# Reordered set-up loads, a split first value sum, TensorE transposes at the end and separate ranks for the first and last steps

## The chip, the cores and the metric

The kernel runs on one core of a Trainium2 chip. The metric is device time in microseconds (us) of one execution, as the median of eight runs. A core has five engines with a queue of instructions each: TensorE (PE in the profile; its weight loads are shown as PEld), VectorE (DVE), ScalarE (ACT), GpSimd (POOL) and SyncE (SP). All transfers of this kernel, the transposing ones too, are issued from SP's queue, one after the other.

## The reference, cut to what matters

Four layers are applied to a sequence of 2048 rows of width 448: A, B, A, B, each added to its input after a layer norm. A is attention with a recurrent memory over 64 segments of 32 rows; B is a gated product with ReLU.

```python
def A(x, mem, Wq, Wk, Wv, Wo):           # 16 heads of 256, 8 memory rows
    for s in range(64):
        h = concat(mem, x[32*s:32*s+32])              # 40 rows
        q, k, v = h @ Wq, h @ Wk, h @ Wv              # per head
        p = softmax(mask(q @ k.T / 16))
        o = (p @ v) @ Wo                              # summed over the heads
        mem = o[:8]                                   # carried to the next segment
        out[s] = o[8:]
def B(x, Wg, Wu, Wd):                    # 1792 wide inside
    return (relu(x @ Wg) * (x @ Wu)) @ Wd
x = x + A(norm(x)); x = x + B(norm(x)); x = x + A(norm(x)); x = x + B(norm(x))
```

Both A layers use the same weights and the same first memory, and so do both B layers.

## The kernel before

**Set-up.** Two products of weights are formed per head, so that no q, k or v is ever built: M = Wq Wk^T (448 x 448 per head, in the tiles `M` and `M3`) and N = Wv Wo (in `N`, 56 blocks of 128 x 448: three blocks of 128 rows for each of 16 heads, numbered `c * 16 + h`, and eight blocks, 48 to 55, that hold the last 64 rows of two heads). `setup` loads Wq, Wk and Wv in head quarters (four heads, 896 KB each) by transposing transfers (`wT`, line 661) and Wo by plain ones (`wo`, line 665), into eight slots of one large tile; Wv and Wo reuse the slots of Wq and Wk. `products` (a quarter at a time) issues the products on TensorE, and ScalarE and VectorE copy each result out of PSUM (`prodE`). The first memory goes through two small loads (lines 654 and 655), one transposing transfer (`mT`, line 656) and a copy on GpSimd (`start_mem`) into `hT`, from which all of step 0 hangs. The slots of the large tile later become the buffers `U` and `UR` and the weights of B.

**Steps.** Step t treats segment t of the first A layer and segment t - 4 of the second together, so there are 68 steps; the first four have the first layer alone and the last four the second alone. In a step, `t_units` multiplies the 40 rows of each layer by M, in ten groups (`tH0`..`tH4` for the last 64 of the 448 rows of the product's inner width, `tF0`..`tF4` for the rest). `s_mem` scores the eight memory rows (`smem`), softmax runs on DVE and ACT (`smx`), `p_t_mem` transposes the probabilities `Pm` on TensorE (`ptm`) and copies them to `PTm`, `u_mem` multiplies them by the rows (`umem`), and `un_mem` sums 56 blocks of N times `UTm` (`unm`, four column groups of the array side by side, 112 matmuls) into the new memory, which `m_t` (`mt`) puts into `hT` for step t + 1. That chain is the recurrence. Beside it, `s_seg` scores the other rows (`sseg`, softmax `ssx` into `Ps`), a transposing transfer (`pts`, line 878) makes `PTs`, `u_seg` multiplies (`useg0`..`useg3`), and `h_nat` supplies the rows in the other layout by a transfer (`hk`, line 884).

**Pairs.** After an odd step, `un` sums 56 blocks of N for the 64 rows of the pair (`un0`..`un3`, or `unc0`..`unc3` where only one layer has rows), `tile_q` normalises the rows (`ln_b`, with a transposing transfer `xBT<-xnB`, line 775) and runs B on them (`glu`: `glH`, `glF`, then the down product `dn` or `dnc`). The second layer's rows of every other pair travel with the memory rows of a later step (`ride`), so a round of four steps repeats: `un` at steps with t % 4 = 1 and `unc` at t % 4 = 3.

**Order.** The order on every engine is made at build time by `_Order.run`: a list scheduler that knows a cost for each operation, starts the one that can go next (within `SLACK` of the earliest), and prefers the highest rank. An operation's rank is its longest path to the end plus `BIAS[kind]`; for TensorE's operations it is a base that falls by 90000 every four steps, plus `BIAS`. `RESERVE[kind]` holds back PSUM banks, and `MODEPEN` is a penalty for a change of the array's tiling. TensorE's kinds carry the step's position in the round:

```python
    def mm(self, kind, fn, cost, rd, wr, mode=FULL):
        self.q.add(f"{kind}.{self.t % 4}", ("pe",), {"pe": (cost + 177.0, cost)}, fn, rd, wr, mode=mode, base=-PERIOD * (self.t // 4))
```

Waits are derived from the reads and writes of each operation, and a queue takes its instructions in the planned order.

Of the kernel before, what the change touches and what calls it, by code (L numbers as in the profile page):

```python
# [6 lines left out]
BF = dt.bfloat16  # L7
# [12 lines left out]
NSEG = 64  # L20
# [8 lines left out]
NP = (NSEG + LAG) // 2  # L29
NSTEP = NSEG + LAG  # L30
# [141 lines left out]
class _Order:  # L172
# [198 lines left out]
BIAS = {"dn.1": -135297.0, "dn.3": -206162.0, "dnE": -604.0, "dnc.1": -674.0, "dnc.3": -136569.0, "glE": -29394.0, "glF0.1": 606.0,  # L371
    "glF0.3": -174334.0, "glF1.1": -142301.0, "glF1.3": -117036.0, "glF2.1": -146133.0, "glF2.3": -132890.0, "glF3.3": -107953.0, "glH0.1":
    5303.0, "glH0.3": -121200.0, "glH1.1": -7321.0, "glH1.3": -104138.0, "glH2.1": -287.0, "glH2.3": -124319.0, "glH3.1": -32499.0,
    "glH3.3": -142572.0, "hk": -25670.0, "init": 17030.0, "lna": -21575.0, "lnaC": 10845.0, "lnaT": 21955.0, "lnb": -26144.0, "mt":
    -18205.0, "mt.0": -22219.0, "mt.1": -153718.0, "mt.2": -1981.0, "mt.3": -108880.0, "mtE": 1853.0, "prodE": 14190.0, "prodM.0":
    -107349.0, "prodN.0": 716.0, "ptm.0": -44820.0, "ptm.1": -17541.0, "ptm.2": -15676.0, "ptm.3": -2267.0, "ptmE": 1947.0, "pts": -1708.0,
    "ride": 22906.0, "rt": -1627.0, "rtT": -18816.0, "smem.0": -2247.0, "smem.1": -3879.0, "smem.2": 10512.0, "smem.3": -126055.0, "smx":
    36486.0, "sseg.0": -14434.0, "sseg.1": 704.0, "sseg.2": -85569.0, "sseg.3": -113319.0, "ssx": 5592.0, "tEm": -574.0, "tEs": -132155.0,
    "tF0.0": 7089.0, "tF0.1": -307.0, "tF0.2": -3560.0, "tF0.3": -18673.0, "tF1.0": 6620.0, "tF1.1": 432.0, "tF1.2": -390.0, "tF1.3":
    -103195.0, "tF2.0": -1468.0, "tF2.1": 9264.0, "tF2.2": 13111.0, "tF2.3": 522.0, "tF3.0": -15739.0, "tF3.1": 2809.0, "tF3.2": -14339.0,  # L380
    "tF3.3": -377.0, "tF4.0": -102794.0, "tF4.1": -105119.0, "tF4.2": 13464.0, "tF4.3": -138946.0, "tH0.0": 3809.0, "tH0.1": 769.0, "tH0.2":
    3829.0, "tH0.3": -14778.0, "tH1.0": 3745.0, "tH1.1": 5395.0, "tH1.2": -4790.0, "tH1.3": -58455.0, "tH2.0": 8825.0, "tH2.1": 8934.0,
    "tH2.2": 2440.0, "tH2.3": 7015.0, "tH3.1": 6664.0, "tH3.2": -373.0, "tH3.3": -115448.0, "tH4.0": -9140.0, "tH4.1": 571.0, "tH4.2":
    21710.0, "tH4.3": -783.0, "umE": -26170.0, "umem.0": 502.0, "umem.1": 7799.0, "umem.2": -1164.0, "umem.3": -14491.0, "un0.1": -1073.0,
    "un0.3": -109778.0, "un1.1": -141926.0, "un1.3": 8423.0, "un2.1": 1237.0, "un2.3": 50702.0, "un3.1": -1050.0, "un3.3": 5387.0, "unc0.1":
    -75505.0, "unc0.3": 3823.0, "unc1.1": -31084.0, "unc1.3": -441.0, "unc2.1": -97666.0, "unc2.3": -112127.0, "unc3.1": -113243.0,
    "unc3.3": -120926.0, "unm.0": -16096.0, "unm.1": -107910.0, "unm.2": 54678.0, "unm.3": -100930.0, "usE": -49724.0, "useg0.0": -76906.0,
    "useg0.1": 49445.0, "useg0.2": -108968.0, "useg0.3": 364.0, "useg1.0": -113562.0, "useg1.1": -97375.0, "useg1.2": -134407.0, "useg2.0":
    -97605.0, "useg2.1": -113.0, "useg2.2": -111646.0, "useg2.3": -127783.0, "useg3.0": -124837.0, "useg3.1": -57685.0, "useg3.2":
    -128034.0, "useg3.3": 3737.0, "w": -19731.0, "wg": -28478.0, "wo": -12799.0, "x": -7455.0, "xE": 41308.0, "xb": -17247.0, "yE": -4405.0,  # L390
    "ys": -6145.0}
RESERVE = {"dn.1": 2, "dn.3": 1, "dnc.1": 2, "dnc.3": 1, "glH0.1": 4, "glH0.3": 1, "glH1.1": 1, "glH1.3": 2, "glH2.1": 1, "glH2.3": 4,
    "glH3.1": 3, "mt.2": 1, "mt.3": 1, "prodM.0": 2, "prodN.0": 1, "ptm.0": 2, "ptm.1": 4, "ptm.2": 4, "ptm.3": 3, "smem.1": 4, "smem.2": 1,
    "smem.3": 2, "sseg.0": 2, "sseg.1": 4, "sseg.2": 4, "tH0.0": 1, "tH0.2": 1, "tH0.3": 2, "tH1.0": 4, "tH1.1": 1, "tH1.2": 2, "tH1.3": 2,
    "tH2.0": 4, "tH2.2": 1, "tH2.3": 2, "tH3.0": 2, "tH3.1": 1, "tH3.3": 1, "tH4.0": 2, "tH4.1": 2, "tH4.2": 3, "tH4.3": 4, "umem.0": 1,
    "umem.1": 3, "umem.2": 3, "un0.1": 3, "un0.3": 3, "unc0.1": 1, "unc0.3": 1, "unc1.1": 2, "unc1.3": 2, "unc2.1": 2, "unc2.3": 2,
    "unc3.1": 2, "unc3.3": 2, "unm.2": 3, "useg0.0": 1, "useg0.1": 2, "useg0.3": 2, "useg1.0": 2, "useg1.1": 1, "useg1.2": 1, "useg1.3": 3,
    "useg2.0": 1, "useg2.1": 3, "useg2.2": 4, "useg2.3": 2, "useg3.0": 2, "useg3.1": 3, "useg3.2": 1, "useg3.3": 2}
SLACK = {"pe": 101.0, "act": 139.0, "dve": 229.0, "pool": 332.0, "sp": 256.0}
PERIOD = 90000.0  # L400
MODEPEN = 41401.0
# [25 lines left out]
def TR(out, src, ident):  # L427
    return (out, src, ident, dict(is_transpose=True))
# [6 lines left out]
class _Kernel:  # L435
# [133 lines left out]
    def mm(self, kind, fn, cost, rd, wr, mode=FULL):  # L569

        self.q.add(f"{kind}.{self.t % 4}", ("pe",), {"pe": (cost + 177.0, cost)}, fn, rd, wr, mode=mode, base=-PERIOD * (self.t // 4))
# [78 lines left out]
    def setup(self):  # L650
        S = self
        S.dma("x", "x0", lambda E: E.dma_start(S.XA[0:64, 0, :], S.x_d[0:64, :]), (), [("XA", 0, 0)])
        mN = S.gT[0:16, :, :].rearrange("p a b -> p (a b)")[:, 0:640]
        S.dma("x", "mN0", lambda E: E.dma_start(mN[0:8, 0:448], S.mem_d), (), [("gT", 0)])
        S.dma("x", "mN1", lambda E: E.dma_start(mN[0:8, 576:640], S.mem_d[:, 384:448]), (), [("gT", 1)])
        S.dma("x", "mT", lambda E: E.dma_start_transpose(S.mTc[:, :, :], mN), [("gT", 0), ("gT", 1)], [("mTc",)], 1160.0, 2400.0)
# [3 lines left out]
        def wT(k, W, q, slow=0.0):  # L660
            S.dma("w", f"w{k}", lambda E: E.dma_start_transpose(S.slot[k], W[:, q * 1024:(q + 1) * 1024]), (), [("slot", k)], 3900.0 + slow,  # L661
                  6200.0 + 1.4 * slow)

        def wo(k, q):
            S.dma("wo", f"w{k}", lambda E: E.dma_start(S.slot[k], S.Wo_d[:, q * 8:q * 8 + 8, :]), (), [("slot", k)], 620.0, 5800.0)
# [36 lines left out]
        for q in range(4):  # L702
            wT(2 * q, S.Wq_d, q)
            wT(2 * q + 1, S.Wk_d, q)
        for q in range(4):
            products(q, 2 * q, 2 * q + 1, True)
        for q in range(4):
            wT(2 * q, S.Wv_d, q, 2300.0 if q else 0.0)
            wo(2 * q + 1, q)
# [7 lines left out]
        for k in range(3):  # L717
            S.dma("wg", f"Wg{k}", lambda E, k=k: E.dma_start(S.Wg[:, k, :], S.Wg_d[k * 128:k * 128 + 128, :]), S.big_keys("Wg"), [("Wg", k)], 500.0, 3000.0)
            S.dma("wg", f"Wu{k}", lambda E, k=k: E.dma_start(S.Wu[:, k, :], S.Wu_d[k * 128:k * 128 + 128, :]), S.big_keys("Wu"), [("Wu", k)], 500.0, 3000.0)
# [465 lines left out]
```

## Time and profile before

| what | us |
|---|---|
| median of 8 runs (lowest, highest) | 1542.08 (1538.39, 1547.73) |
| the profiled execution | 1540.43 |
| its span, first to last instruction | 1538.4 |
| PE busy in the span | 1473.8 |
| ACT busy, DVE busy | 811.0, 698.7 |
| first product of the set-up starts on PE | 10.85 |
| first `un_mem` ends | 86.5 |
| first sum of `unc`'s form (step 3) starts | 137.80 |
| last sum of `un` ends | 1521.6 |

Matmuls overlap in the array, so a PE that is shown busy is not always at its peak. The median is what is forecast; the execution in the profile was 1.65 us faster than it.

### The profile page before, as it was taken

What the parts mean: (1) busy time and instruction counts of PE and PEld (TensorE: products, weight loads), DVE (VectorE), ACT (ScalarE), POOL (GpSimd) and SP (SyncE); (2) the same over time, 40 slices, a digit from 0 to 9 for tenths busy, and PEclk for the clock granted to TensorE, in tenths of its full rate; (3) what the DMA queues carried; (4) which work ended last, traced back from release to release, by engine and by line L of the source; (5) the groups of instructions that cost most, each with busy time, mean ns of one, the idle gap of its engine ahead of it and who ended that gap; (6) DMA issues with size and microseconds to landing.
All of it is one profiled execution on the core that took longest, in us unless ns stands there. A gap on an engine that the chain in (4) does not pass through costs nothing.

```text
span 1538.4 us, 72169 instructions
## 1 busy us (share of the span) xinstructions
PE 1473.8 (96%) x33352; PEld 1157.5 (75%) x33352; DVE 698.7 (45%) x1851; ACT 811.0 (53%) x2421; POOL 90.9 (6%) x142
## 2 busy tenths in 40 slices
PE   5789999999999999999999999999999999999998
PEld 2467777887878778887877778787877788787775
DVE  4334444443535455344535454344535444353443
ACT  5544545555555646555555545555554555545543
POOL 2000000000000000000000000000000000000000
PEclk9999999999999999999999999999999999999999
DMA  9851111011111111111112112111112201221111
GB/s 222 179 146 33 23 29 28 19 29 29 32 20 34 25 32 26 23 29 29 29 24 34 24 26 29 23 33 28 29 21 34 28 19 29 28 31 19 31 26 23
DMA packets 187549, 59.76 MB, mean 39 GB/s; under 512 B 176344, under 2 KB 186352, under 8 KB 187248
## 3 DMA queue, kind: packets, MB, share of 16 engines
q1 hardware_dynamic: 187248, 55.15, 19.7%
q8 instruction: 262, 4.29, 1.2%
q14 instruction: 39, 0.32, 0.1%
HBM read 10.33 MB, written 1.84 MB: 8 GB/s over the span
## 4 chain that ended last, share of the span: by engine, by line
PE 87%; DMA 6%; DVE 3%; ACT 2%; SPq 1%; issue 1%; POOL 0%; POOLq 0%
PE P L134 87%; DMA PTs<-Ps 4%; DMA xBT<-xnB 1%; SPq L661 1%; ACT big L599 1%; DMA mTc<-gT 1%; ACT XH L943 0%; DMA big<-in_A_Wk_dram 0%; DVE X L946 0%; DMA stg<-xnA 0%; DVE xnB L757 0%; DVE stat L823 0%; DVE stat L820 0%; DVE big L600 0%; DVE hB L1077 0%
## 5 line engine op out<-in xcount | busy, mean ns | idle before, releaser
L134 PE MATMUL P<-hT,Mw 128*128 128x80 bf16 (+1 forms) x11424 | 422.3, 200 | 0.4 <-ACT Mw L599 0.4
L134 PEld LDWEIGHTS P<-hT,Mw 128*128 128x128 bf16 x11424 | 403.2, 100 | 9.3 <-ACT Mw L599 0.5
L134 PE MATMUL P<-Nw,big 128*64 128x448 bf16 (+1 forms) x1904 | 283.7, 353 | 0.5
L599 ACT ACTIVATE TTm<-P 128x96 bf16<-128x96 f32 (+2 forms) x612 | 147.9, 242 | 239.3 <-PE P L134 231.1
L599 ACT ACTIVATE TTs<-P 128x384 bf16<-128x384 f32 (+2 forms) x596 | 268.6, 451 | 0.2
L134 PE MATMUL P<-xBT,big 128*128 128x128 bf16 (+3 forms) x3808 | 213.9, 217 | 3.0 <-DMA xBT<-xnB 3.0
L134 PEld LDWEIGHTS P<-Nw,big 128*64 128x64 bf16 (+1 forms) x1904 | 136.1, 104 | 107.0 <-issue 3.4
L134 PEld LDWEIGHTS P<-xBT,big 128*128 128x128 bf16 (+1 forms) x3808 | 182.9, 98 | 24.8 <-issue 10.2
L134 PE MATMUL P<-Nw,UTm 128*32 128x224 bf16 x7504 | 193.6, 261 | 2.8 <-ACT UTm L599 2.8
L134 PEld LDWEIGHTS P<-Nw,UTm 128*32 128x32 bf16 x7504 | 176.2, 97 | 20.5 <-issue 11.5
L599 ACT ACTIVATE big<-P 128x512 bf16<-128x512 f32 (+1 forms) x371 | 176.4, 536 | 23.4 <-PE P L134 22.4
L820 DVE TENSOR_REDUCE stat<-P 128x8 f32<-128x320 f32 (+3 forms) x135 | 46.2, 351 | 212.3 <-PE P L134 212.0
L600 POOL COPY UTm<-big 128x896 bf16<-128x896 bf16 x56 | 52.3, 934 | 1109.2 <-PE P L134 1109.2
L600 DVE CAST TTm<-P 128x64 bf16<-128x64 f32 (+3 forms) x68 | 15.5, 228 | 198.1 <-PE P L134 197.9
L946 DVE TENSOR_TENSOR X<-P,XH 32x224 bf16<-32x224 f32 x134 | 51.1, 381 | 116.4 <-ACT XH L943 113.7
L600 DVE CAST big<-P 128x512 bf16<-128x512 f32 (+1 forms) x141 | 90.3, 655 | 27.5 <-PE P L134 25.3
L134 PE MATMUL P<-PTs,hK 64*128 64x512 bf16 (+1 forms) x640 | 84.2, 337 | 18.9 <-DMA PTs<-Ps 15.3
L134 PE MATMUL P<-big,hB 128*128 128x448 bf16 (+1 forms) x476 | 98.7, 353 | 1.5 <-DVE hB L1077 1.5
L134 PE MATMUL P<-hT,M 64*128 64x80 bf16 (+1 forms) x3808 | 92.4, 196 | 7.8 <-POOL hT L600 6.2
L1076 ACT ACTIVATE gT<-P 128x512 bf16<-128x512 f32 (+2 forms) x136 | 70.7, 522 | 51.9 <-PE P L134 47.6
L134 PEld LDWEIGHTS P<-hT,M 64*128 64x128 bf16 x3808 | 74.7, 96 | 30.7 <-issue 11.7
L1077 DVE TENSOR_TENSOR hB<-gT,P 128x512 bf16<-128x512 bf16 (+2 forms) x136 | 76.5, 589 | 41.8 <-PE P L134 37.6
(85 smaller groups left out, 1155.6 us busy)
## 6 DMA issues: line engine op xcount, KB each, us to landing
big<-in_A_Wo_dram SPq DMA_DIRECT2D x4, 896.0 KB, 6.9
XA<-in_A_x_dram SPq DMA_DIRECT2D x32, 56.0 KB, 2.4
out_dram<-ys SPq DMA_DIRECT2D x32, 56.0 KB, 2.0
big<-in_B_W_down_dram SPq DMA_DIRECT2D x2, 784.0 KB, 9.3
big<-in_B_W_gate_dram SPq DMA_DIRECT2D x3, 448.0 KB, 5.0
big<-in_B_W_up_dram SPq DMA_DIRECT2D x3, 448.0 KB, 6.6
PTs<-Ps SPq DMA_TRANSPOSE x68, 2.6
hK<-hT SPq DMA_TRANSPOSE x68, 2.6
```

The costliest lines, as they stand in the source:

```text
L134: ins = E.matmul(out, lhsT=lhsT, rhs=rhs, **kw)
L599: return E.activation(out(), src(), ACT.Copy)
L600: return E.tensor_copy(out(), src())
L661: S.dma("w", f"w{k}", lambda E: E.dma_start_transpose(S.slot[k], W[:, q * 1024:(q + 1) * 1024]), (), [("slot", k)], 3900.0 + slow, 6200.0 ...
L820: S.dve(kind, lambda E: E.tensor_reduce(st[:, so:so + n], src(), AX.X, ALU.max), w, rd, [(pre, 0)])
L946: S.dve("xE", lambda E, r=r, r2=r2, c=c: E.tensor_tensor(S.X[r, c], T.b()[r, 0:224], S.XH[r2, :], ALU.add), 224, T.res((j,)) + [("XH",)], ...
L1076: S.act("glE", lambda E, G=G, k=k, w=w: E.activation(S.gT[:, k % 2, 0:w * n], G.b()[:, 0:w * n], ACT.Relu), w * n, G.res(), [("gT", k % 2)])
L1077: S.dve("glE", lambda E, V=V, k=k, w=w, a=a: E.tensor_tensor(S.hB[:, a:a + w, 0:n], S.gT[:, k % 2, 0:w * n].rearrange("p (i x) -> p i x", ...
```

## The change

Four edits, and new values in all tables of the scheduler.

1. In `setup`, x0, the two memory loads and the memory's transposing transfer get a kind of their own (`mem`) with a high rank. Each of the 16 weight loads has its own kind (`wq0`..`wo3`), and the costs that the scheduler assumes for transfers are altered.
2. The first `un_mem` (t = 0) is issued as four operations over head quarters. Each waits for the 14 blocks of N of its quarter instead of all 56. The other steps sum in the same new order of blocks, in one operation.
3. The last `PTs<-Ps` (step 67) and the last `xBT<-xnB` (pair 33) are no longer transfers: four transposes on TensorE into one PSUM bank and one copy on VectorE.
4. Kinds on TensorE are numbered 4 to 7 in steps 0 to 3, 8 to 11 in steps 64 to 67, and 0 to 3 in between.

```diff
-BIAS = {"dn.1": -135297.0, "dn.3": -206162.0, "dnE": -604.0, "dnc.1": -674.0, "dnc.3": -136569.0, "glE": -29394.0, "glF0.1": 606.0,
...
+BIAS = {"dn.1": -104633.0, "dn.3": -214049.0, "dn.9": -140910.0, "dnE": -786.0, "dnc.11": -139309.0, "dnc.3": 13831.0, "dnc.5": -27812.0,
...
-SLACK = {"pe": 101.0, "act": 139.0, "dve": 229.0, "pool": 332.0, "sp": 256.0}
+SLACK = {"pe": 101.0, "act": 142.0, "dve": 226.0, "pool": 0.0, "sp": 124.0}
 PERIOD = 90000.0
-MODEPEN = 41401.0
+MODEPEN = 42065.0
...
-        self.q.add(f"{kind}.{self.t % 4}", ("pe",), {"pe": (cost + 177.0, cost)}, fn, rd, wr, mode=mode, base=-PERIOD * (self.t // 4))
+        part = 4 if self.t < 4 else 8 if self.t >= NSEG else 0
+        self.q.add(f"{kind}.{self.t % 4 + part}", ("pe",), {"pe": (cost + 177.0, cost)}, fn, rd, wr, mode=mode, base=-PERIOD * (self.t // 4))
...
-        S.dma("x", "x0", lambda E: E.dma_start(S.XA[0:64, 0, :], S.x_d[0:64, :]), (), [("XA", 0, 0)])
+        S.dma("mem", "x0", lambda E: E.dma_start(S.XA[0:64, 0, :], S.x_d[0:64, :]), (), [("XA", 0, 0)])
...
-        S.dma("x", "mN0", lambda E: E.dma_start(mN[0:8, 0:448], S.mem_d), (), [("gT", 0)])
-        S.dma("x", "mN1", lambda E: E.dma_start(mN[0:8, 576:640], S.mem_d[:, 384:448]), (), [("gT", 1)])
-        S.dma("x", "mT", lambda E: E.dma_start_transpose(S.mTc[:, :, :], mN), [("gT", 0), ("gT", 1)], [("mTc",)], 1160.0, 2400.0)
+        S.dma("mem", "mN0", lambda E: E.dma_start(mN[0:8, 0:448], S.mem_d), (), [("gT", 0)])
+        S.dma("mem", "mN1", lambda E: E.dma_start(mN[0:8, 576:640], S.mem_d[:, 384:448]), (), [("gT", 1)])
+        S.dma("mem", "mT", lambda E: E.dma_start_transpose(S.mTc[:, :, :], mN), [("gT", 0), ("gT", 1)], [("mTc",)], 1200.0, 2500.0)
...
+        if q == NP - 1:
+            S.transposed("lnbT", S.xnB[:, :], 512, S.xBT[:, :, :].rearrange("p a b -> p (a b)"), [("xnB",), ("xnB", 0), ("xnB", 1)], [("xBT",)])
+            return
...
+        if t == NSTEP - 1:
+            S.transposed("pts", S.Ps[:, :, :].rearrange("p a b -> p (a b)"), 512, S.PTs[:, :, :].rearrange("p a b -> p (a b)"), [("Ps",)], [("PTs",)])
+            return
...
+    def transposed(self, kind, src, n, dst, rd, wr):
+
+        S = self
+        T = S.tile()
+        S.mm(kind, lambda: [TR(T.b().bitcast(BF)[:, c:c + 128], src[:, c:c + 128], S.ident[:, :]) for c in range(0, n, 128)],
+             n // 128 * S.pitch(128), rd + [("ident",)], T.res())
+        S.cp(kind + "E", lambda: dst, lambda: T.b().bitcast(BF)[:, 0:n], n, T.res(), wr, speed=1.9, eng=("dve",))
...
+    OS = [[c * 16 + h for c in range(3) for h in range(4 * q, 4 * q + 4)] + [48 + 2 * q, 49 + 2 * q] for q in range(4)]
...
+        rd = [("UTm", 0), ("UTm", 1), ("UTmr",)]
+        if t == 0:
+            for q in range(4):
+                S.mm("unm", lambda q=q: mms(7 * q, 7 * q + 7), 7 * S.pitch(224), rd + [("N", o) for o in S.OS[q]], T.res(), mode=COLS4)
+        else:
+            S.mm("unm", lambda: mms(0, 28), 28 * S.pitch(224) + 18.0, rd, T.res(), mode=COLS4)
```

## The prediction

> **What bounds the kernel now.** I read the page's busy times and chain first, then what PE waited for, then the first 100 us and the last 20 us in fine windows.
>
> ```profile
> PE 1473.8 (96%) x33352; PEld 1157.5 (75%) x33352; DVE 698.7 (45%) x1851; ACT 811.0 (53%) x2421; POOL 90.9 (6%) x142
> ...
> PE 87%; DMA 6%; DVE 3%; ACT 2%; SPq 1%; issue 1%; POOL 0%; POOLq 0%
> ```
>
> PE holds 87% of the chain that ended last. Time can come off only where PE stands still, runs at half clock, or changes tiling needlessly. PE's waits over the whole span:
>
> ```profile
> PE P L134 <- DMA big<-in_A_Wk_dram: 15.9, 4, 10.9
> PE P L134 <- DMA PTs<-Ps: 15.3, 15, 1.9
> PE P L134 <- POOL hT L600: 6.2, 2, 5.8
> PE P L134 <- issue: 3.4, 3, 2.0
> ```
>
> (columns: total us, times, longest). The first line is the weights of the set-up, the third the first memory. The second is not the ends: 14 of its 15 waits lie between 140 and 1480 us, one in each round of four steps. Set-up, first SP's timeline (columns: start us, us, what):
>
> ```profile
> 33.13 0.52 SPq L654 DMA_DIRECT2D gT<-in_A_mem_dram  x1
> 36.78 3.96 SPq L656 DMA_TRANSPOSE mTc<-gT  x1
> 49.65 14.48 SPq L661 DMA_TRANSPOSE big<-in_A_Wv_dram  x3
> ```
>
> Then windows of 4 us (columns: PE, PEld, DVE, ACT, POOL busy, granted clock, DMA share, GB/s):
>
> ```profile
> 40.00:44.00 4.00, 0.00 (x0) 0.00 (x0) 0.07 (x1) 0.32 (x2) 0.00 (x0) 1.00 1.20 362
> 44.00:48.00 4.00, 2.50 (x30) 1.35 (x31) 0.23 (x1) 0.77 (x2) 0.22 (x1) 0.61 1.07 225
> 48.00:52.00 4.00, 3.56 (x98) 2.62 (x96) 0.67 (x3) 2.98 (x12) 0.00 (x0) 0.96 0.35 89
> 56.00:60.00 4.00, 1.95 (x10) 0.55 (x8) 0.78 (x2) 1.16 (x3) 0.00 (x0) 0.82 1.28 189
> ```
>
> The memory's transfer is issued at 36.78, behind 2.7 MB of Wo, and takes 8.4 us to land. PE has placed step 0's first units ahead of the last M products, so it stands still from 39.65 to 45.5. That also keeps a slot occupied: the last Wo waits for PE, and the DMA share falls to 0.35 at 48 to 52. The tail, by the timeline:
>
> ```profile
> 1524.57 1.31 PE L134 MATMUL P<-big,hB 128*128 128x448 bf16 x6 [1.51 <-DVE hB L1077]
> 1527.49 5.75 PE L134 MATMUL P<-xBT,big 64*128 64x64 bf16 x112 [1.61 <-DMA xBT<-xnB]
> ```
>
> and a window in it:
>
> ```profile
> 1527.00:1533.00 6.00, 5.51 (x111) 5.24 (x112) 1.23 (x4) 1.30 (x4) 0.00 (x0) 0.50 0.10 22
> ```
>
> Two gaps on PE, and the last gated products run at clock 0.50.
>
> **Set-up loads and the split sum.** From 35.95 (last quarter of M starts) to the end of the first `un_mem`, about 86.5, PE's windows leave 8.6 us idle: 0.35, 4.0, 1.5, 0.44, 2.05 and 0.29 in the windows from 36, 40, 44, 48, 56 and 64. Half clock adds 1.4 us (10 product matmuls in 3.18 us, where 64 later ones took 11.33, so 0.177 each) and 1.6 (24 in 5.89 against 4.25). That is 11.7 us; the work itself is about 39 us.
>
> With the memory first, the stall of 5.85 and its half clock go, and Wo3's hold-up with them. What is moved costs at the front: SP issues the two memory loads (0.52 and 0.28) and the transpose, before the bulk of the weights. The transpose's issue is between 1.2 (every small transpose at an uncrowded queue, such as `stg<-xnA` at 9.40) and 3.96 (where it is now); I take 1.2, because only one weight load is ahead of it. So Wq and Wk land 2.0 us later (bounds 0.8 and 4.8; below 0.8 only if the backlog on the queue hides an issue). This is paid in full: PE waited 1.7, 2.0 and 1.3 us for each next quarter, so nothing covers it. POOL's copy into `hT` then waits for no late transfer; on POOL's queue it stands behind memsets that end at 8.5.
>
> The split adds three waits and some tiling changes, 0.1 to 0.2 us each: 0.4. Its gain is bounded by the sum itself, 2.9 us, of which three quarters (2.1) can lie before the last N blocks. But PE is busy there (64 product matmuls without a gap, 71.20 to 82.5), so on a PE-bound stretch moving them brings nothing; it helps only in a wait for Wv. I book 0 for it: the cover is PE's own work, and without it the end is Wv3's arrival plus 5.6 of products.
>
> That arrival: DMA is full from 4 to 48 and from 52 to 66, idle for about 3 between. Without the hole the last weights land near 63 to 65. PE, from 38, with 5.3 of M, 5.3 of units and 16.6 of N, wants the last quarter at 65. Just in time.
>
> One stall I don't book as gone: 2.05 us at 56.2, with 1.6 of half clock behind it, whose releaser the profile calls "issue". It follows a burst of 168 short matmuls under a full DMA. The burst and the DMA load stay, so it may return; between 0 and 3.7 I take 1.8.
>
> Sum: 11.7 - 2.0 - 0.4 - 1.8 = 7.5 us off (bounds 3 and 11).
>
> **Steps 0 to 3 with their own ranks.** From 86.6 to 104 PE stands still 5 us and loses 2.5 at clock 0.5 (112 matmuls of `un_mem` in 4.43 us against 2.87 elsewhere). But this is the recurrence with one layer and no finished pair, so there is little to fill it. Loads of B's weights run until 94 and are moved forward with the rest. I book 1 us (bounds 0 and 3).
>
> **The tail.** `xBT<-xnB` takes 2.44 us from `xnB` to the first matmul. In its place: one transpose of 0.23 (row of `ident,Pm`), three more at the pitch of 128 columns (88 matmuls in 4.62 us, 0.053 each), a copy, and three handovers of 0.05. The trace has no bf16 copy of 512 elements from PSUM; the nearest are 0.22 for 128 bf16 and 0.69 for 512 f32, and half the slope of the f32 rows gives 0.45. Together 1.0, so 1.45 off.
>
> The half clock: 112 matmuls in 5.75 us, 51 ns each, would be about 3.2 at full clock: 2.5. The row: the clock is 1.00 until 1526 and 0.50 from 1527 to 1533, after gaps of 1.51 and 1.61 us. The Trainium skill, "TensorE: Matmul & The Clock Gate", Part 1, has the gate close after an idle window of about 3.4 us; neither gap is that long, so by it there would be no half clock to win. The row decides: two shorter gaps were enough. Part 4 of that page speaks against this edit: transposes do not count as PE-busy for the gate, so by it they would not hold the clock, and the tail would win only 1.45 and something for `Ps`. I side with the full clock, because the gap of 3.4 us on DVE and ACT (XF at 1521.66 to xnB at 1525.04) can be filled with ordinary matmuls: the transfer of the last `PTs` (1511.06 to about 1513.7) shrinks to 1.0, so the last `useg` and `unc` can go 1.6 earlier and leave more of pair 32's products for that gap. For the gap of 1.51 I book 0.7. The eight transposes and their tiling changes cost 0.2. If nothing fills the gap, the 2.5 come back.
>
> Sum: 1.45 + 2.5 + 0.7 - 0.2 = 4.5 off (bounds 1.5 and 5.5).
>
> **The rounds.** All ranks are new, also of steps 4 to 63. The `unc` sums mark the rounds:
>
> ```profile
> 137.80 5.49 PE L134 MATMUL P<-Nw,big 128*64 128x448 bf16 x56
> 1357.71 5.49 PE L134 MATMUL P<-Nw,big 128*64 128x448 bf16 x56
> ```
>
> They are 14 rounds apart, 87.14 us each. Each round has one wait of about 1 us for `PTs`, and PE's idle from 140 to 1480 is about 24 us, 1.6 per round. No row shows what other ranks do, and one more wait of 0.5 is as possible as one less, so the bounds are +8 and -15. I take a quarter of the `PTs` wait, 0.26 a round, 4 us, because ranks freed from serving the ends have only that stretch to serve.
>
> Against the profiled execution (span 1538.4 and 2.0 around it, 1540.43): 7.5 + 1 + 4.5 + 4 = 17.0 us off, 1523.4. It was 1.65 below the median of 1542.08; carried to the median, 1525.
>
> **The rivals.**
>
> *Rounds much better* (0.12). The `PTs` wait vanishes in every round: 15 x 1.0 instead of 4, so 1514, or less if other waits fall with it. For it: the wait recurs at one place in the order. Against: products of the earlier pair run out there, and PE's total is unchanged.
>
> *The ends give little* (0.14). SP's queue is the bound of the set-up: the transpose issues at 3.96, "issue" returns in full, and the clock stays at half in the tail. Set-up 3, tail 1.5, rounds 0: 1537.5; with a little from the rounds, 1534. For it: DMA shares of 1.1 to 1.3 while PE waits. It also covers edits that are not on the path.
>
> *Slower* (0.04). The new ranks place `useg` or `glu` so that PE meets one more wait in each round. From 13.0/15 = 0.87 us a round the ends' 13.0 are eaten; at 1.2 us, the size of the `PTs` waits, 15 x 1.2 = 18, or 1547. Against: nothing in the edits lengthens a round's chain, and a wait of that size in each round would be as plain in a plan as the `PTs` wait is in this trace.
>
> *No change that shows* (0.02), the same at about 0.9 a round: 1542.
>
> **How the numbers follow.** About 0.2%, 3.1 us, is what a measurement of this kernel can tell from no change. The likeliest case (0.68) gives 1525, from 1517 to 1533 by its bounds. The range of 1510 to 1534.5 takes in most of the better rounds and half of the small gain. Faster 0.93 (the likeliest, the better rounds, nearly all of the small gain), same 0.03, slower 0.04.
>
> **What would show it.** Right: `mTc<-gT` issued before 10 us; no PE gap over 1 us between 38 and 48; first `un_mem` ending near 79; first `unc` sum near 129; rounds of 86.9; the last gated products at clock 1.00 in about 3.2 us; PE's wait for `xBT` gone at the end. Wrong: the wait for Wk or Wv grown by over 3 us, 0.50 after 1510, or a round over 87.6.

## The result, and the profile after

The changed kernel takes 1534.45 us (median of 11 runs, 1529.01 to 1536.75) where the kernel before took 1542.64 in the same series: ratio 0.9943, 95% interval 0.993 to 0.9956. It is faster by about 8 us where 17 were forecast. A second series, further down, gave 0.9959 (0.9945 to 0.9972).

PE's work fell by 5.4 us and its share stayed where it was (page, busy time of the engine, share of the span, instructions):

```profile
PE 1468.4 (96%) x33360; PEld 1154.9 (76%) x33360; DVE 721.6 (47%) x1911; ACT 798.2 (52%) x2363; POOL 92.5 (6%) x142
```

DVE has 60 instructions more and ACT 58 fewer: the new order gives DVE more of the copies out of PSUM. What PE waited for over the span (total us, times, longest):

```profile
PE P L134 <- DMA big<-in_A_Wk_dram: 16.0, 2, 15.1
PE P L134 <- DMA PTs<-Ps: 12.7, 13, 1.5
PE P L134 <- DVE X L1010: 7.1, 10, 1.3
PE P L134 <- DMA big<-in_A_Wq_dram: 3.1, 1, 3.1
```

The wait for the first memory (6.2 us before) is gone. The wait for `PTs` shrank from 15.3 to 12.7, but the wait for `X`, VectorE's last step of the memory sum, doubled from 3.5 to 7.1. SP's timeline shows that the memory is not the very first (start us, us, what):

```profile
0.73 7.42 SPq L704 DMA_TRANSPOSE big<-in_A_Wq_dram  x2
8.21 0.60 SPq L695 DMA_DIRECT2D XA<-in_A_x_dram  x1
...
9.73 3.37 SPq L704 DMA_TRANSPOSE big<-in_A_Wk_dram  x1
13.22 1.14 SPq L699 DMA_TRANSPOSE mTc<-gT  x1
```

Two quarters of Wq go ahead of it and of the first quarter of Wk, so that the first product waits for Wk until 15.13 instead of 10.85; the memory's transpose issues in 1.14 us at 13.22, not in 3.96 at 36.78. PE's stall of 5.85 us for the memory is gone. A wait of 3.1 us for a quarter of Wq ends at 38.04, with half clock behind it (windows; PE, PEld, DVE, ACT, POOL busy, granted clock, DMA share, GB/s):

```profile
36.00:40.00 4.00, 1.96 (x9) 0.67 (x10) 0.41 (x2) 0.70 (x2) 0.00 (x0) 0.62 1.20 256
40.00:44.00 4.00, 4.00 (x13) 1.66 (x12) 1.40 (x6) 2.55 (x7) 0.91 (x2) 0.52 1.12 251
```

At the end there is no gap on PE any more (timeline, and the window around it):

```profile
1517.61 0.39 PE L134 MATMUL P<-ident,xnB 128*128 128x128 bf16 x4
1517.83 0.92 PE L134 MATMUL P<-big,hB 128*128 128x448 bf16 x4
1518.68 3.35 PE L134 MATMUL P<-xBT,big 64*128 64x64 bf16 x112
```

```profile
1518.00:1522.00 4.00, 4.00 (x118) 3.31 (x118) 2.71 (x6) 1.21 (x4) 0.00 (x0) 1.00 0.09 18
```

The last gated products take 3.35 us at clock 1.00, where they took 5.75 at 0.50. The sums of `unc`'s form that the prediction used as marks start at

```profile
126.66 1.51 PE L134 MATMUL P<-Nw,big 128*64 128x448 bf16 x14
...
1350.69 1.14 PE L134 MATMUL P<-Nw,big 128*64 128x448 bf16 x10
```

which is 14 rounds of 87.43 us, against 87.14 before. Rounds became longer.

To compare all kernels I cut each profiled execution at the starts of `un_mem` (read from the trace: the first, the second, those of steps 7 and 59), at the start of the last `un` sum and at the end. The fifth column holds exactly 13 rounds.

| kernel | to first un_mem | step 1 | to step 7 | 13 rounds | to last un sum | to the end | span | ratio of runs to before |
|---|---|---|---|---|---|---|---|---|
| before | 83.7 | 16.0 | 119.4 | 1134.2 | 162.8 | 22.3 | 1538.4 | 1 |
| changed | 74.5 | 15.3 | 117.6 | 1138.9 | 162.3 | 18.6 | 1527.2 | 0.9943 |
| changed, second series | 72.8 | 16.8 | 119.3 | 1140.2 | 162.3 | 18.6 | 1530.0 | 0.9959 |
| swap | 74.8 | 19.2 | 119.0 | 1134.8 | 160.9 | 18.6 | 1527.3 | 0.9907 |
| cast_late | 74.4 | 16.4 | 118.8 | 1133.9 | 160.3 | 18.6 | 1522.4 | 0.9910 |
| cast_act | 73.1 | 19.5 | 121.7 | 1132.6 | 160.7 | 18.6 | 1526.2 | 0.9901 |
| before_swap | 81.7 | 17.3 | 121.9 | 1141.5 | 163.2 | 19.9 | 1545.5 | 1.0025 |
| spread | 74.0 | 14.6 | 125.7 | 1135.1 | 160.6 | 18.6 | 1528.6 | 0.9893 |
| spread2 | 73.2 | 18.1 | 122.6 | 1133.9 | 160.7 | 18.6 | 1527.1 | 0.9902 |
| late | 73.4 | 21.6 | 121.7 | 1141.0 | 162.4 | 18.6 | 1538.7 | 0.9958 |
| early | 74.9 | 19.4 | 120.8 | 1140.7 | 162.0 | 18.6 | 1536.4 | 0.9942 |
| unsplit | 75.2 | 18.4 | 119.3 | 1140.1 | 161.9 | 18.6 | 1533.5 | 0.9941 |
| tail_dma | 73.5 | 18.0 | 119.7 | 1141.3 | 168.9 | 22.0 | 1543.4 | 1.0015 |
| shift | 73.1 | 20.5 | 121.9 | 1140.3 | 163.4 | 18.6 | 1537.8 | 0.9960 |
| swap_shift | 72.3 | 21.5 | 121.5 | 1137.5 | 163.1 | 18.6 | 1534.5 | 0.9929 |
| before_shift | 81.3 | 19.9 | 121.3 | 1134.6 | 162.3 | 22.5 | 1541.9 | 0.9986 |
| before_tail | 82.4 | 17.2 | 119.2 | 1137.3 | 161.8 | 20.4 | 1538.3 | 0.9993 |

Two things are to be kept in mind with it. The changed kernel's profiled execution was its fastest in both series (1529.01 and 1531.75 against medians of 1534.45 and 1538.02), so its rows flatter it by 5 to 6 us; before's (1540.43) stood 2 us under its median. And step 1 varies most from one execution to another: from 15 to 22 us in kernels with the changed kernel's order of PE, most of which alter nothing there.

### The profile page after: what moved, and what is told of

It reads as the page before. It is cut to its first block, busy times and chain, and to the rows that moved or that the text cites. A ratio compares the mean times of both kernels' runs of the same rounds, so it can differ in the third digit from the quotient of the medians.

```text
span 1527.2 us, 72243 instructions
## 1 busy us (share of the span) xinstructions
PE 1468.4 (96%) x33360; PEld 1154.9 (76%) x33360; DVE 721.6 (47%) x1911; ACT 798.2 (52%) x2363; POOL 92.5 (6%) x142
## 4 chain that ended last, share of the span: by engine, by line
PE 83%; DVE 6%; DMA 5%; ACT 2%; SPq 2%; issue 1%; POOL 0%
PE P L134 83%; DMA xBT<-xnB 2%; SPq L704 2%; DMA PTs<-Ps 2%; ACT big L642 1%; DVE big L643 1%; DVE xnA L799 1%; DVE X L1010 1%; DMA big<-in_A_Wq_dram 1%; DVE stat L868 1%; DVE stat L865 0%; ACT XH L1007 0%; DVE stat L792 0%; DVE XA L1170 0%; DVE ys L1173 0%
## 5 line engine op out<-in xcount | busy, mean ns | idle before, releaser
L642 ACT ACTIVATE TTm<-P 128x96 bf16<-128x96 f32 (+2 forms) x593 | 143.8, 242 | 247.4 <-PE P L134 241.3
L642 ACT ACTIVATE TTs<-P 128x384 bf16<-128x384 f32 (+2 forms) x582 | 263.2, 453 | 0.4 <-DVE TTm L643 0.2
L642 ACT ACTIVATE big<-P 128x512 bf16<-128x512 f32 (+1 forms) x346 | 169.4, 548 | 17.9 <-PE P L134 16.9
L643 DVE CAST TTm<-P 128x64 bf16<-128x64 f32 (+3 forms) x87 | 19.8, 228 | 279.5 <-PE P L134 279.4
L643 DVE CAST big<-P 128x512 bf16<-128x512 f32 (+1 forms) x166 | 98.7, 620 | 22.4 <-PE P L134 20.5
L1010 DVE TENSOR_TENSOR X<-P,XH 32x224 bf16<-32x224 f32 x134 | 51.1, 381 | 117.6 <-ACT XH L1007 115.0
L134 PE MATMUL P<-PTs,hK 64*128 64x512 bf16 (+1 forms) x640 | 85.1, 337 | 20.2 <-DMA PTs<-Ps 12.7
L1007 ACT ACTIVATE XH<-P 64x224 f32<-64x224 f32 x67 | 23.6, 352 | 136.6 <-PE P L134 136.4
```

The lines of the kernel that those rows point to most:

```text
L134: ins = E.matmul(out, lhsT=lhsT, rhs=rhs, **kw)
L642: return E.activation(out(), src(), ACT.Copy)
L643: return E.tensor_copy(out(), src())
L1007: S.act("xE", lambda E: E.activation(S.XH[64:128, :], T.b()[64:128, 0:224], ACT.Copy), 224, T.res(BOTQ), [("XH",)])
L1010: S.dve("xE", lambda E, r=r, r2=r2, c=c: E.tensor_tensor(S.X[r, c], T.b()[r, 0:224], S.XH[r2, :], ALU.add), 224, T.res((j,)) + [("XH",)], ...
```

## The experiments

The diffs below are shortened: lines with a comment sign, and names such as `move` or `copy_1`, put in words what the edit does.

### Where the rounds lost: VectorE's order

In each round one step (t % 4 = 1) has a pair's normalisation beside the memory sum. Measured from the start of `un_mem` to the matmul that selects the new memory (`P<-selm,X`), this step took at least 4.47 us before (mean of 13 rounds 5.00). In the changed kernel it took at least 5.26 in the eleven rounds that have the new order of copies described below, and 5.27 in the mean of all 13; I call the least value the floor. What PE waited for in just these 13 rounds (total us, times, longest), before and in the changed kernel:

```profile
PE P L134 <- DMA PTs<-Ps: 13.4, 13, 1.9
...
PE P L134 <- DVE X L946: 1.1, 2, 0.5
```

```profile
PE P L134 <- DMA PTs<-Ps: 11.4, 11, 1.5
PE P L134 <- DVE X L1010: 5.3, 6, 1.3
```

VectorE's timeline of one such step, before (start, us, what):

```profile
610.05 0.61 DVE L757 TENSOR_SCALAR xnA<-XA,stat 128x448 bf16<-128x448 bf16 x2
610.68 0.42 DVE L600 CAST big<-P 128x256 bf16<-128x256 f32 x1
611.15 0.80 DVE L946 TENSOR_TENSOR X<-P,XH 32x224 bf16<-32x224 f32 x2
```

and in the changed kernel, with GpSimd's one operation there:

```profile
598.42 0.72 DVE L643 CAST big<-P 128x256 bf16<-128x256 f32 x2
599.17 0.63 DVE L1173 TENSOR_TENSOR ys<-P,XB 64x448 bf16<-64x448 f32 x1
599.83 1.22 DVE L799 TENSOR_SCALAR xnA<-XA,stat 128x448 bf16<-128x448 bf16 x2
601.08 0.79 DVE L1010 TENSOR_TENSOR X<-P,XH 32x224 bf16<-32x224 f32 x2
```

```profile
599.94 1.08 POOL L643 COPY UTm<-big 128x896 bf16<-128x896 bf16 x1 [16.71 <-PE P L134]
```

The new order puts two copies ahead of `ys` and `xnA`. `xnA` is thereby late enough to meet GpSimd's copy of the riding rows, and takes 1.22 us instead of 0.61; `X` starts 4.09 us after the sum's start instead of 3.30. In the step shown `PTs` landed later still, so PE waited for `PTs` and not for `X`. Where `PTs` comes early, as in the next round, PE waits for `X`:

```profile
689.00 0.79 DVE L1010 TENSOR_TENSOR X<-P,XH 32x224 bf16<-32x224 f32 x2
689.85 0.39 PE L134 MATMUL P<-PTs,hK 64*128 64x512 bf16 x2 [1.32 <-DVE X L1010]
```

The same place before, in a round with an early `PTs`:

```profile
1311.31 0.39 PE L134 MATMUL P<-PTs,hK 64*128 64x512 bf16 x2 [0.53 <-DVE X L946]
```

**swap**: the changed kernel, with before's order of these copies in eleven rounds. The order is altered between planning and emission; PE's order stays.

```diff
         self.q.run()
+        # each un_mem with t % 4 == 1: of VectorE's two copies (usE) ahead of ys and xnA,
+        # one to ScalarE, ahead of XH; the other behind xnA
+        _swap(self.q)
         self.q.emit()
```

> The changed kernel with one difference: in eleven rounds (steps 13 to 53 with t % 4 = 1) ScalarE and VectorE take the evacuations around the sum of the memory values in the order that the kernel before has there. One copy of 256 elements goes from VectorE to ScalarE, the other stands behind the normalised rows xnA. TensorE's order is untouched. Theory A (VectorE's order is what lengthened the rounds: xnA runs beside GpSimd's copy, takes 1.22 instead of 0.61 us, and the new memory rows X come 0.8 us late, so that the selection matmul starts no earlier than 5.27 us after the sum): its earliest start goes back to 4.47 us, the mean to about 4.9, xnA to 0.61, and the span loses 4 to 5 us; ratio to before about 0.991. Theory B (the rounds are longer only because instruction fetches fall differently beside the transfer of PTs): the start stays near 5.27, no change from the changed kernel, ratio 0.994.

This is theory A of the expectations. 1529.17 us, ratio 0.9907 (0.989 to 0.9924). The floor was 4.47 again, the 13 rounds 1134.8, and no piece of `xnA` took over 0.40 us. PE's order is the same in both traces, matmul by matmul. The part of the change outside the rounds is therefore worth about 14 us, and the new order of the copies took some 5 of them back.

**cast_act** and **cast_late** move one of the two copies only.

```diff
+        move(copy_1, before=XH); copy_1.engine = act      # cast_act
...
+        move(copy_2, before=X)                            # cast_late: behind xnA, still VectorE
```

> The changed kernel with one of VectorE's two copies ahead of xnA given to ScalarE in eleven rounds (swap gave one to ScalarE and put the other behind xnA). In the changed kernel the selection matmul starts 5.27 us behind un_mem at the least, in swap 4.47. Theory A1 (each copy ahead of X costs its 0.36 us): floor about 4.9, half of swap's gain, 1531.5 to 1532.5 us, ratio 0.9925. Theory A2 (it is the overlap of xnA with GpSimd's copy, xnA 1.22 us for two where 0.61 is its time alone): xnA starts 0.36 earlier and is half out of the overlap, floor 4.6 or below, nearly all of swap's gain, 1529.5 to 1530.5 us, ratio 0.991.

> The changed kernel with one of VectorE's two copies moved behind xnA, still on VectorE and still ahead of X, in eleven rounds; ScalarE's work is as in the changed kernel. Theory A1 (VectorE's work ahead of X counts): nothing is gained, floor 5.2, 1534 to 1536 us, ratio 0.9945. Theory A2 (the overlap counts): xnA back to about 0.61 for two, X 0.6 us earlier or as soon as ScalarE's half is there, floor 4.7, 1530.5 to 1531.5 us, ratio 0.9915.

cast_act: 1528.57 us, 0.9901 (0.9885 to 0.9917), floor 4.47. cast_late: 1528.97 us, 0.9910 (0.9892 to 0.9928), floor 4.77. In cast_late VectorE has as much to do ahead of `X` as in the changed kernel, and nearly the whole gain came. So it is mainly the overlap that cost the time; of the floor's 0.79 us, the 0.30 that cast_late kept belong to the second copy itself. `xnA` by the view of that tile, 140 to 1340 us (minimum, median, maximum in ns), first the changed kernel, then cast_late:

```profile
L799 DVE TENSOR_SCALAR xnA<-XA,stat x54: 294/396/914, 152.2 to 1301.7; 128x448 bf16<-128x448 bf16 x27, 128x64 bf16<-128x64 bf16 x27
```

```profile
L830 DVE TENSOR_SCALAR xnA<-XA,stat x54: 293/342/397, 154.5 to 1299.4; 128x448 bf16<-128x448 bf16 x27, 128x64 bf16<-128x64 bf16 x27
```

Its second piece, 64 columns, takes 0.29 us alone and up to 0.91 when GpSimd's copy has started before it. In the step shown first it ran from 600.14 to 601.05, and GpSimd's copy ended at 601.02; in all eleven rounds the piece ended 0.03 to 0.04 us after that copy. So it seems to have stood until the copy was through, not to have run slowly. In cast_late the piece starts 0.14 us before GpSimd's copy and takes 0.29. The Trainium skill, "SBUF — State Buffer", section "Who interferes with whom", says just this: VectorE in a two-port mode, which `tensor_scalar` can enter, and GpSimd share a pair of ports as an exclusive lock, and the later one blocks for the whole instruction. The trace agrees, at 0.6 us a time.

**before_swap**: the kernel before, with the changed kernel's order of the copies in thirteen rounds.

```diff
+        copy_1.engine = dve; move(copy_1, before=ys); move(copy_2, before=ys)
```

> The kernel before with the changed kernel's order of evacuations in thirteen rounds: VectorE takes a second copy, and both stand ahead of ys and xnA. Theory (this order is what lengthened the rounds): the wait of PE for X grows in each, floor from 4.47 to 5.2, round 87.25 to 87.7, 4 to 6 us slower than before, ratio 1.003. Rival (swap gained by something else that came with its order): no change, ratio 1.000.

1546.65 us, ratio 1.0025 (1.0014 to 1.0035): 3.8 us slower, floor 5.26, longest `xnA` piece 0.912 us, 13 rounds 1141.5 instead of 1134.2, PE's wait for `X` in them 5.5 us instead of 1.1. The order alone costs it, in either kernel. PE's own new order shows no effect on the rounds: with before's copies the 13 rounds took 1134.2 to 1137.3 under before's ranks and 1133.9 to 1137.5 under the new ones (swap, spread, spread2, swap_shift); with the changed copies 1141.5 and 1138.9 to 1141.3.

### PTs and the fetches of instructions

The other thing that PE meets in that step is the transfer `PTs<-Ps`. In the changed kernel's trace, between 140 and 1480 us, 30 of these transfers landed 2.44 to 2.78 us after issue; in 32 a packet of the instruction queue (16 KB, about 1 us) starts between issue and landing, and these took 3.3 in the median, 4.3 at most, though 11 of them were not delayed. Before: 26 at 2.39 to 2.73, 35 with such a packet at 3.9 in the median. No transfer without a packet took longer than 2.78. So the wait for `PTs` seems to come and go with the place of a fetch. Three kernels shift the fetches by 64 extra matmuls ahead of the first product:

```diff
         S.ln_a(0)
+        for n in range(2):
+            S.q.add("dummy", ("pe",), ..., lambda: [MM(bank, ident, ident[:, 0:32]) for _ in range(32)], ...)
```

> The changed kernel with 64 small matmuls added on TensorE before the first product, where TensorE is idle; their result is not used. They move the places in the program at which TensorE's next 16 KB of instructions are fetched by half a fetch. Theory B: the fetch packets move against the transfers of PTs at t % 4 = 1, from 0.4 to 0.8 and 1.9 to 2.1 us after their issue to about 0.4 or none in turn; TensorE's wait for PTs in those rounds falls from 0.88 us on average to under 0.4. Theory A: that wait may fall, but the selection matmul still starts 5.27 us after the sum in each round, because X is late on VectorE, so the time stays within 1.5 us of the changed kernel, ratio 0.994.

> Both edits in one kernel: VectorE's and ScalarE's order of the kernel before in eleven rounds, and 64 matmuls ahead of the first product. If the two waits hide each other (A sets a floor of 5.27 us, the late PTs come on top of a floor of 4.47), only both edits together free the rounds: selection matmul 4.5 to 4.7 us after the sum, 0.6 to 0.8 us a round less than the changed kernel, 7 to 9 us in all, ratio 0.989. If A alone is right it equals the first of these runs; if B alone is right it equals the second.

> The kernel before with the same 64 matmuls ahead of the first product and nothing else. Theory B: the transfers of PTs at t % 4 = 1 meet fewer fetch packets, TensorE's wait for them falls from 0.96 to under 0.4 us a round, and since X is not late in this kernel, the span loses about 0.4 us in each of 13 rounds, 4 to 6 us, ratio 0.997. If the fetch packets have no part in it, the wait stays at about 1 us and the ratio is 1.000.

shift: 1538.61 us, 0.996 (0.9947 to 0.9974). swap_shift: 1532.87, 0.9929 (0.9912 to 0.9947). before_shift: 1541.53, 0.9986 (0.9976 to 0.9997). The rounds moved by no more than 0.2 us each. PE's wait for `PTs` in the step of the sum, mean of 13, was 0.80 in shift (0.87 in the changed kernel), 0.96 in swap_shift (0.94 in swap) and 0.73 in before_shift (0.92 before); under 0.4 was expected of shift and before_shift. The waits changed rounds instead of going. Fetches come by the count of instructions (256 of PE's, weight loads included, from one packet to the next in the median), and a shift meets others. before_shift came out just faster than before; the other two are no faster than the kernels that they were made from. swap_shift is 3.7 us slower than swap by the medians; in the profiles its step 1 took 2.3 us more and its 13 rounds 2.7. The connection with the fetches (theory B) holds in the traces, but a shift doesn't use it.

### Step 1: where set-up time is given back

swap stood still twice in step 1 (PE's timeline):

```profile
84.06 0.47 PE L134 MATMUL P<-hT,M 64*128 64x40 bf16 x24 [1.97 <-issue]
...
89.69 0.63 PE L134 MATMUL P<-hT,TTs 128*128 128x40 bf16 x13 [1.95 <-issue]
```

with clock 0.50 from 90 to 96. This is a stretch of short matmuls, some 40 in a microsecond, while B's weights fill the DMA engines. **spread** moves the last five of those loads back.

```diff
+    # SP: Wu0, Wu1, Wu2 behind step 1's second PTs; Wd0, Wd1 behind step 2's hK
```

> The changed kernel with the order of evacuations as in swap (before's order in eleven rounds), and B's up and down weights issued later on SP: up behind step 1's second transfer of PTs (near 93 us instead of 75 to 83), down behind step 2's hK (near 100 instead of 84). In swap PE stood still twice for nearly 2 us in 82 to 90 us with no releaser ('issue') while those weights took all DMA engines, and the clock was at 0.50 behind that. Theory C (instruction fetches of PE queue behind the weight loads there): the two stalls go, step 1 takes 15 to 16 us instead of 19.2, and the time is 3 to 5 us below swap, 1524.5 to 1526 us, ratio 0.988. Rival (the stalls are the program's own, or move along with the loads): step 1 stays at 19 us and the time at 1529 us, ratio 0.991.

1528.03 us, ratio 0.9893 (0.9874 to 0.9912). Step 1 took 14.6 us and the two stalls were gone; but a stall came back beside the loads' new place, and the stretch to step 7 grew from 119.0 to 125.7:

```profile
104.59 0.28 PE L134 MATMUL P<-hT,TTm 128*128 128x40 bf16 x5 [2.74 <-issue]
```

**spread2** issues the same five loads one at a time.

```diff
+    # SP: Wu0, Wu1 behind PTs of step 1 and its successor, Wu2 behind step 2's hK, Wd0 behind the next PTs, Wd1 behind step 3's hK
```

> As spread, but B's up and down weights are issued one load at a time, each behind a transfer of steps 1 to 3 (up behind PTs of step 1 and its successor and behind step 2's hK, down behind PTs of step 2 and step 3's hK). In spread step 1 took 14.6 us without the two stalls, but a stall of 2.7 us on PE came at 101.9, beside the loads in their new place. Theory C (a fetch of PE's instructions waits behind a long run of loads): without long runs no stall with releaser 'issue' over 1 us is left between 75 and 125 us, the fourth un_mem starts by 124.5 us instead of 127.2, and the time is 1525 to 1526 us, ratio 0.9875. Rival (any load beside these steps costs its stall): a stall of 1.5 us or more stays behind one of the loads, 1528 us, ratio 0.9893.

1528.9 us, 0.9902 (0.988 to 0.9923), with stalls of 1.97 us at 80.5 and 1.85 at 118.3: the rival. Neither kernel is distinguishable from swap.

What PE stood for can be read from the DMA packets in the traces. The 17 traces hold 28 stalls of over 1 us with releaser 'issue', and in every one PE went on 1.28 to 1.58 us after the end of a 16 KB packet of the instruction queue. In 22 of them that packet came late: PE had started 319 to 533 instructions (weight loads included) since the packet before, where the median is about 256 and, from 140 us on, 95% come by 310. In swap's first stall it was 512, in spread's 416. The other six are second stalls soon behind a late packet. So PE seems to have run out of instructions. The weight loads are the likeliest reason: from the 256th instruction to the start of the late packet the DMA share was 0.9 to 1.6, and the stall followed the loads. A kernel without loads in this stretch was not tried.

### The memory's place, the weights' order, the split sum

**late**: the memory's loads go back to nearly where they were, ahead of the first Wo and just behind it.

```diff
+    # SP: mN0, mN1 ahead of Wo0, mT behind it; the rest as in the changed kernel
```

> The changed kernel with the memory's loads as late on SP as in before: the two small loads ahead of the first Wo and the transposing transfer right behind it; all else in the changed kernel's order. Theory (the memory's place carries most of the set-up's gain): POOL's copy into hT waits about 5 us for it again and PE stands still near 36 to 42 us; the first un_mem starts 4 to 7 us later than the 74.5 us of the changed kernel, and the time is 1538.5 to 1541 us, ratio 0.9975. Rival (the gain comes from the order of the weights and of PE): 1534 to 1536 us, ratio 0.9945 or below.

1536.41 us, ratio 0.9958 (0.9944 to 0.9972), beside 0.9959 for the changed kernel in the same series. The theory fell. Its memory reached `hT` at 39.70 (GpSimd's timeline), and PE asked for it at 45.08:

```profile
39.70 0.22 POOL L674 COPY hT<-mTc 128x40 bf16<-128x40 bf16 x1 [31.16 <-DMA mTc<-gT]
```

```profile
45.08 0.62 PE L134 MATMUL P<-hT,M 64*128 64x40 bf16 x36
```

In the new PE order step 0's units stand behind all M products. That, not the earlier transfer, is what took away the stall of 5.85 us. (In late the transfer stands behind one load of Wo and issues in 1.16 us; behind three, as before, it issued in 3.96 and landed after 8.4, and the copy into `hT` came at 45.23. Even that would have kept PE only some 0.4 us from 45.08 on.)

**early**: the first product's weights go first.

```diff
+    # SP: Wq1, Wk1, x0, mN0, mN1, Wq0, mT, ... (was Wq0, Wq1, x0, mN0, mN1, Wk1, mT, ...)
```

> The changed kernel with three set-up loads in another order on SP: the second quarters of Wq and Wk first, then x, the two memory transfers, and only then the first quarter of Wq. In the changed kernel the first product waits 15.1 us for Wk, 4.2 us longer than before. Theory (the first product's weights stand behind other issues): the first product starts near 11 us, and if nothing else bounds the set-up the whole is 3 to 4 us faster, 1531 us, ratio 0.992. Rival (the later weights, which all follow in one queue, bound the set-up): PE waits for them a few products later instead, 1534 to 1535 us.

1535.5 us, 0.9942 (0.9927 to 0.9957). The first product started at 10.27 and the next Wk was then waited for 6.39 us. First `un_mem` at 74.9, as without it (74.5): the rival; the queue of weights bounds the set-up.

**unsplit**: the first `un_mem` as one operation again.

```diff
-        if t == 0:
-            for q in range(4): S.mm("unm", ... 7 blocks ..., rd + [N of quarter q])
+        S.mm("unm", ... 28 blocks ..., rd + Nkeys)
```

> The changed kernel with the first un_mem as one operation that waits for all of N, as before. The trace of the changed kernel shows its four parts back to back, with nothing between them. Theory (the split is worth nothing): 1534 us, within 1.5 us either way, ratio 0.994. Rival (the parts let PE begin the sum earlier, and their order carries part of the earlier start): 1537 us or more, ratio 0.996 or above.

1535.54 us, 0.9941 (0.9926 to 0.9957): the split is worth nothing.

**after_2**: the changed kernel once more.

> The changed kernel again, unaltered, for a second profile beside the first, which was its fastest execution. If a typical execution loses in step 1 what the first profile did not lose (as in swap, shift and others, 18 to 20 us from the first to the second un_mem instead of 15.3), this one shows 18 us or more, stalls with releaser 'issue' of 1.5 us or more between 78 and 92, and a span of about 1532; if the first profile was the rule, 15.3 us and a span of 1527. Rounds (14 of them) 87.6 us either way; median 1534.5, ratio 0.9943.

1538.02 us, 0.9959 (0.9945 to 0.9972). Step 1 took 16.8 us with one stall of 1.05: between the two expectations. The profiled executions of this kernel were its luckiest both times.

### The tail

**tail_dma** takes the transposes out of the changed kernel, **before_tail** puts them into the kernel before.

```diff
-        if t == NSTEP - 1:            # tail_dma; the same for q == NP - 1
-            S.transposed("pts", ...); return
...
+        if t == NSTEP - 1:            # before_tail; the same for q == NP - 1
+            S.transposed("pts", ...); return
```

> The changed kernel with its third edit undone: PTs of step 63 and xBT of the last pair come by a DMA transpose again, everything else as in the changed kernel. If the tail term of the prediction holds, the end from the last memory sum on grows by 4 to 5.5 us: about 1538.5 to 1540 us, ratio to the kernel before 0.997; the last gated products take over 5 us again, partly at clock 0.50, and PE waits for the transfer of xBT. If instead the end was set by something that the transposes don't touch, 1534 to 1535 us, ratio 0.9943.

> The kernel before with the third edit alone: the last PTs and the last xBT by TensorE transposes and a copy, ranks of before, so that the order is that of before until step 65. Theory (the tail term, 4.5 us off, bounds 1.5 to 5.5): ratio 0.997, about 1539.5 us where before has 1544; from the start of the last un sum to the end 18 to 19 us instead of 22.3, last gated products at clock 1.00. Rival (the tail's gain in the changed kernel came from its new ranks): ratio 0.999 or above.

(The step 63 of the first expectation is the last one, step 67, which treats segment 63.) tail_dma: 1546.69 us, 1.0015 (1.0006 to 1.0025), 0.7% slower than the changed kernel. Its order was planned anew behind step 63 with ranks that were made for transposes: PE waited 5.86 us for `xBT`, and 6.6 us more went between step 59 and the last sum. before_tail: 1541.4 us, 0.9993 (0.9979 to 1.0007). From the last sum to its end it took 20.4 us instead of 22.3, and 1.0 less up to that sum; its 13 rounds, in the very order of before, happened to take 3.1 more. The gain of the transposes under the old ranks is thus 3 us in that profile and not established by the ratio.

Of the 3.7 us between before and the changed kernel in this stretch, 2.4 rest on the clock, and the clock is not the same in every execution. before_swap has the same tail as before, with the same gaps:

```profile
1534.05 1.31 PE L134 MATMUL P<-big,hB 128*128 128x448 bf16 x6 [1.51 <-DVE hB L1110]
1536.96 3.35 PE L134 MATMUL P<-xBT,big 64*128 64x64 bf16 x112 [1.61 <-DMA xBT<-xnB]
```

Gaps of 1.51 and 1.61 us, and the products ran at clock 1.00 in 3.35 us; in before they ran at 0.50 in 5.75. In the two other traces with the transfer the second gap was longer and the clock fell during these products: 4.81 us in before_shift (gaps of 1.51 and 2.75) and 4.72 in tail_dma (5.86). In all 13 traces with the transposes no gap in this stretch is over 0.5 us, and the products took 3.35 at 1.00. The kernels with transposes and the changed ranks took 18.6 us for this stretch in every profile. At full clock, before_swap with the transfer took 19.9 and before_tail with the transposes 20.4: under the old ranks the transposes by themselves gained nothing there, only the clock.

## Why the prediction was wrong

**The rounds: this step failed.** It booked "a quarter of the `PTs` wait, 0.26 a round, 4 us" off, with the reason that "ranks freed from serving the ends have only that stretch to serve", and held against a longer round that "nothing in the edits lengthens a round's chain". The wait for `PTs` in the 13 rounds did shrink, from 13.4 to 11.4 us, but PE's wait for `X` in them rose from 1.1 to 5.3. From step 1's end to the last `un` sum the rounds and what stands between them got 2.4 us longer in the fastest execution, and the 13 rounds alone 4.7 (1138.9 against 1134.2; 6.0 in the second series). Of these 4.7, PE's longer waits make 2.7; the rest is spread over its busy time and small gaps. That is an error of 9 to 10 us in one term, as large as the whole miss against the median (9.5). The kernel swap shows the size from the other side: with the order of eleven rounds' copies as before, the time is 1529.17 (0.9907), and the prediction without its rounds term would have been 1529 (0.9915). That these two agree so closely is luck, since the other terms came for other reasons.

The rival of a longer round was priced at one more wait in PE's order; what came was a later `X` on VectorE, from a collision with GpSimd: the new ranks and costs altered the order on VectorE too, and for the rounds the prediction looked at PE's alone. The profile of before had the pieces: `xnA` at 610.05, GpSimd's copy at 610.79, 0.13 us after `xnA` ended. The prediction's reading that each round has one wait of about 1 us for `PTs` was too even: in the step of the sum it was none in three of 13 rounds and up to 1.88 in others.

**Set-up: size near by luck, reason wrong.** 7.5 us were booked and the first `un_mem` starts 9.2 earlier. The other profiles have it at 81.3 to 82.4 with before's set-up and at 72.3 to 75.2 with the changed one, so some 8.5 us are usual. But late shows that the place of the memory's transfer was not needed for it. PE's order, and with it the order of the weights, did it; these two were not tried apart. The stall that "I don't book as gone" went from its place: with the changed order no stall of its kind of over 1 us begins before 77.9 us in any trace. But such stalls came in step 1, where 4 us of the gain were lost in an execution such as swap's (19.2 against 15.3) and 6 in late's (21.6). The 2.0 us for later weights were 4.3 (first product at 15.13 instead of 10.85), which early proves harmless: the wait just moves to the next Wk.

**The split at 0: right** (unsplit). **Own ranks of steps 0 to 3, 1 us:** the stretch from the first `un_mem` to step 7 took 2.5 us less in the first profile and 0.7 more in the second: not separable from step 1's scatter.

**The tail: right in the sum, not in its surety.** 4.5 us were booked; up to the last sum 0.5 and from there 3.7 came, 4.2. The copy took 0.42 us where 0.45 was estimated, the gated products 3.35 where 3.2 was. But 2.4 us of it is a half clock that the same gaps brought in one execution and not in another; in the four traces with the transfer the products took 5.75, 4.81, 4.72 and 3.35, so the share to be expected is smaller than 2.4. I let one row decide against the Trainium skill's "TensorE: Matmul & The Clock Gate", Part 1, and the row was right in that gaps below 3.4 us can be enough (before, before_shift), wrong in that they always are (before_swap). That part also says that the gate's window is free-running, and the two tails with equal gaps fit that better than any rule by the length of a gap. Its Part 4, that transposes don't keep the clock up, was not put to a test: ordinary matmuls follow 0.22 us after the transposes' start.

**From profile to median.** The prediction carried the profiled execution to the median by 1.65 us. For the changed kernel that distance was 5.4 and 6.3, which hid more of the gain. In its profile it gained 11.2 us of span: 11.7 up to step 7 and 4.2 behind step 59, less 4.7 in 13 rounds.

Of the marks that would show it wrong, one applied at the border: rounds of 87.6 (87.61 by `un_mem`, 87.43 by the `unc` sums). Another applied to the letter, without a loss: the first wait for Wk grew from 10.9 to 15.1 us, the waits for Wk together did not (15.9, 16.0). Of the marks that would show it right, two failed: `mTc<-gT` was issued at 13.22, not before 10, and the rounds did not fall to 86.9. The kernels with the copies in the former order beat both: about 1529 us, 0.989 to 0.991, which is 0.3 to 0.7 per cent below the changed kernel's two ratios.

## What to carry to other kernels

When all ranks of a scheduled kernel are new, the stretch that repeats most is the one to price, and a gain there may not be booked from the intention: two copies of 0.36 us each, put ahead on an engine that isn't the bottleneck, cost 13 rounds about 5 us. Before moving work between VectorE, ScalarE and GpSimd, look at which VectorE operation will then stand beside a GpSimd copy. A clock row of one execution is one throw; a term that rests on it needs a second profile, or a smaller size.

## What the hardware showed that was not expected

- A VectorE normalisation of 64 columns that takes 0.29 us takes 0.91 when a GpSimd copy of 1.08 us has started 0.2 us before it; both then end within 0.04 us of each other.
- A transposing transfer that lands in 2.4 to 2.8 us lands in 3.3 to 3.9 in the median when a 16 KB packet of the instruction queue falls in between.
- PE stood up to 3.7 us with no releaser in stretches of short matmuls, most often beside full weight loads. In all 28 such stalls of over 1 us it went on 1.28 to 1.58 us after the end of a 16 KB packet of the instruction queue.
- Equal gaps of 1.51 and 1.61 us gave a granted clock of 0.50 in one execution and 1.00 in another.
